# A transformer block on one Trainium2 core: a buffer of its own for a third partial sum, residual adds on another engine, earlier partial sums, earlier statistics of the first tile

## The chip, the core and the metric

The kernel runs on one core of one Trainium2 chip. The metric is the device time of that core in microseconds (us). A kernel is run several times in a job, beside the kernel before on the same chip; medians and ranges are over those runs. The engines are called PE (matmul; PEld is its weight load), DVE (the vector engine), ACT (the scalar engine), POOL (GpSimd) and SP (which here only issues transfers).

## The reference

One block: a modulation vector from `c`, LayerNorm, a two-dimensional Fourier filter, a residual, LayerNorm again, a SwiGLU feed-forward, a residual. x is 2048 x 640 in bf16, the feed-forward is 1728 wide.

```python
mod = (_silu(c) @ w_mod).reshape(c.shape[0], 6, 1, -1)        # sa, ca, ga, sb, cb, gb
h = _layernorm(x) * (1 + ca) + sa
x = x + ga * irfft2(rfft2(h) * (w_r + 1j * w_i))
h = _layernorm(x) * (1 + cb) + sb
x = x + gb * ((silu(h @ w_gate) * (h @ w_up)) @ w_down)
```

The kernel does the Fourier transforms as matmuls with tables. Both parts of the feed-forward use a Strassen-Winograd scheme: seven products for eight, paid for with sums on DVE. The rows are taken in chunks of 2, 4, 4, 4 and 2 tiles of 128. The first chunk is done plainly, the other four in seven *down pairs* (two tiles each): 2 + 2 + 2 + 1.

## The kernel before

`[...]` marks cuts. First the head: the statistics of a tile, and the order in which the first tiles are issued. The order matters: in the trace of this kernel POOL scales tile 0's table (L372, from `gscale(0)`) at 10.61 us, behind the power for tile 1 (L357, 9.94 to 10.50), which stands before it in the program, although tile 0's own power had ended at 8.34.

```python
def stats(t):
    if t in BN:                                   # by bn_stats on DVE (tiles 0 and 1 among them)
        for k in range(2):
            nc.vector.bn_stats(bn6a[:, k, :], x_sb[:, t, 320 * k:320 * k + 320])
        nc.vector.bn_aggr(mv[:, t, :], bn6a[:])
    else:
        gram_stats(t)
    [...]                                         # variance on DVE
        nc.gpsimd.tensor_tensor(rstd[:, tt], vtmp[:, tt], mhalf[:, 0:len(us)], ALU.pow)

def gscale(t):                                    # first table of tile t times its rstd, on POOL
    [...]
    nc.gpsimd.tensor_scalar(Gs[:, 0:2, :], Gtab[:, tg], rstd[:, t:t + 1], float(D) ** 0.5, ALU.mult, ALU.mult)
    nc.gpsimd.tensor_scalar(Gs[:, 2, :], Gtab[:, tg, 1, :], rstd[:, t:t + 1], -float(D) ** 0.5, ALU.mult, ALU.mult)

for r in range(4):
    nc.vector.tensor_scalar_mul(Rs[:, 1, r, :], Rp[:, 4, :], mask4[:, r:r + 1])   # waits for tab_R
[...]
t1(0)                                             # transposes of tile 0
stats(0)
[...]
t1(1)
stats(1)
gscale(0)
[...]
gscale(1)
nc.gpsimd.tensor_copy(sc_rep[:], sc_f[:].unsqueeze(2).to_broadcast([P, NC5, 128]))
[...]
s1(0, Zs.pop(0), Gss.pop(0))                      # PE: needs gscale(0)
```

Then the down pair. X, Y, Z and W are PSUM banks; S1 to S4 are DVE sums of the activations (`a_sum`), T1 to T4 prepared sums of weights. X collects three partial sums one after another, and each is copied out by ACT before the next.

```python
g21b, g22b = (rL.cut(1024 * i, [512]) for i in range(2))
cps_ = [rL.cut((2560, 10496, 0, 1280)[i], [320], F32) for i in range(4)]

def a_sum(ATc, j, i, ks=slice(0, HK)):            # one of S1..S4, for the 128-column blocks ks of 7
    [...]
    tt = nc.vector.tensor_tensor

def down_pair(ATc, t, j, nxt):
    [...]
    last = t + 2 == NT
    prod(X, A11, B11, True, ks=range(0, 6))
    prod(Z, A12, B21, True, ks=range(0, 2))
    prod(X, A11, B11, stop=True, ks=range(6, HK))
    nc.scalar.copy(cps_[0], X)
    nc.gpsimd.tensor_tensor(xa[:, 0:320], xa[:, 0:320], cps_[0], ALU.add)
    [...]
    prod(Y, S1, T1, True, True)
    nxt(0)
    nc.scalar.copy(cps_[1], Y)
    prod(X, S2, T2, stop=True)
    nxt(1)
    nc.scalar.copy(cps_[2], X)                    # the third partial sum
    nc.gpsimd.tensor_tensor(xb[:, 320:640], xb[:, 320:640], cps_[1], ALU.add)
    nc.gpsimd.tensor_tensor(xa[:, 320:640], xa[:, 320:640], cps_[2], ALU.add)
    [...]                                         # four more products and the stores

def h_sums(ci):                                   # DVE sums for the gate-up of the next chunk
    [...]
    tt(t1, b11, b12, ALU.subtract)
    tt(t3, b22, b12, ALU.subtract)
    tt(t2, b22, t1, ALU.add)
    tt(t4, t2, b21, ALU.subtract)
    nc.vector.tensor_scalar_mul(t2, t2, -1.0)
```

`cps_[2]` at byte 0 of `rL` lies over `g21b` and the start of `g22b`, the activated gates of the gate-up stage that goes before.

## Time and profile before

| | before |
|---|---|
| median of 3 runs | 255.58 us (255.17 to 255.83) |
| span of the profiled execution | 254.3 us |
| PE busy / DVE busy / POOL busy | 96% / 83% / 30% |
| PE idle before a third product of a down pair | 2 x 0.4 us |
| first matmul of the last pair to the end of the span | 11.42 us |

The page of the kernel before begins with span, busy us, share and number of instructions of each engine.

```profile
span 254.3 us, 6460 instructions
PE 245.3 (96%) x2513; PEld 200.1 (79%) x2513; DVE 212.0 (83%) x517; ACT 162.3 (64%) x299; POOL 77.4 (30%) x123
```

PE is all but full, and the change leaves its work as it is. So a gain can come only from a gap of PE, and there are few. The list of waits of the kernel before names them (PE's output, line, what it waited for, us in total, times, longest):

```profile
PE psum L897 <- ACT rL L919: 0.8, 2, 0.4
PE psum L570 <- DMA rM<-in_w_mod_dram: 0.7, 1, 0.7
...
PE psum L971 <- POOL rW L784: 0.4, 1, 0.4
...
PE psum L897 <- DVE rE L854: 0.3, 1, 0.3
```

The first line is the down pairs, the last is the last pair. The timeline of the kernel before around one of those two pairs (start, duration, engine, line, operation, out<-in, form; in brackets the idle time before it and what ended it):

```profile
177.26 1.00 DVE L1062 TENSOR_TENSOR rX<-rH,rL 128x512 bf16<-128x512 bf16 x1
177.29 1.12 PE L897 MATMUL psum<-rA,rE 128*128 128x320 bf16 x7
178.35 0.42 ACT L919 COPY rL<-psum 128x320 f32<-128x320 f32 x1 [1.39 <-DVE rX L1062]
178.83 1.11 PE L897 MATMUL psum<-rE 128*128 128x320 f16 x7 [0.42 <-ACT rL L919]
178.83 0.77 PEld L897 LDWEIGHTS <-rE 128*128 128x128 f16 x6 [0.62 <-issue]
```

ACT could have copied the third partial sum (L919) much earlier, but it waits until DVE (L1062) has read `g22b`, which lies in the same bytes. PE then waits for the copy.

The last pair on the kernel before's DVE timeline: the sums L854 to L860 stand between PE and its products.

```profile
244.96 0.75 DVE L854 TENSOR_TENSOR rE<-rX 128x128 f16<-128x128 bf16 x1
245.63 0.68 DVE L856 TENSOR_TENSOR rE<-rE,rX 128x768 f16<-128x768 f16 x2
246.24 1.35 DVE L860 TENSOR_TENSOR rE<-rX,rE 128x768 f16<-128x768 bf16 x2
247.51 1.38 DVE L858 TENSOR_TENSOR rE<-rX 128x768 f16<-128x768 bf16 x2
```

And on its POOL timeline, the residual adds that run beside them:

```profile
244.77 0.86 POOL L910 TENSOR_TENSOR rM<-rM,rL 128x320 f32<-128x320 f32 x1 [17.83 <-ACT rL L909]
246.62 0.88 POOL L920 TENSOR_TENSOR rM<-rM,rL 128x320 f32<-128x320 f32 x1 [0.99 <-ACT rL L916]
247.95 0.86 POOL L921 TENSOR_TENSOR rM<-rM,rL 128x320 f32<-128x320 f32 x1 [0.45 <-ACT rL L919]
```

Two sums (a row x2 has two) take 0.68 us where POOL is quiet, and 1.35 and 1.38 where a POOL add lies over them. The head, in the kernel before's POOL timeline and then its weight-load timeline:

```profile
9.94 0.56 POOL L357 TENSOR_TENSOR rstd<-vtmp,mhalf 128x1 f32<-128x1 f32 x1 [1.61 <-DVE vtmp L352]
10.61 0.48 POOL L372 TENSOR_SCALAR rE<-rE,rstd 128x256 bf16<-128x256 bf16 x1
```

```profile
11.13 0.10 PEld L396 LDWEIGHTS <-rE 128*128 128x128 bf16 x1 [0.23 <-POOL rE L372]
11.60 0.10 PEld L397 LDWEIGHTS <-rE 128*128 128x128 bf16 x1 [0.37 <-POOL rE L373]
```

The scaling of tile 0's table (L372) stands behind the power for tile 1 (L357), and the first s1 products wait for it twice.

### The profile page before, as it was taken

The numbers are of one execution on the slowest core, as the hardware profiler recorded it, in microseconds if no ns is written. First come the engines' busy times: TensorE is split into PE (matmuls) and PEld (weight loads), VectorE is DVE, ScalarE is ACT, GpSimd is POOL, SyncE is SP. The second block draws the span as 40 slices with busy tenths as digits, with TensorE's granted clock in tenths as the row PEclk, the third lists the DMA queues.
The fourth block names the chain that finished last, engine by engine and source line by source line (L and its number), as shares of the span: only waits on it lengthen the run. The fifth ranks groups of instructions, "written<-read, shape, count | busy, mean of one in ns | idle before, by whom it ended". The sixth has DMA issues, their size and how long they took to land.

```text
span 254.3 us, 6460 instructions
## 1 busy us (share of the span) xinstructions
PE 245.3 (96%) x2513; PEld 200.1 (79%) x2513; DVE 212.0 (83%) x517; ACT 162.3 (64%) x299; POOL 77.4 (30%) x123
## 2 busy tenths in 40 slices
PE   8999998989999999999999999999999999999994
PEld 3678868989789888688877778886678887679962
DVE  2889898978898997779997997879985888993895
ACT  3678757978788686778862577674357765235630
POOL 7487785954022804000003900002220000440021
PEclk9999999999999999999999999999999999999999
DMA  6999999999999899600005020004210000211001
GB/s 220 396 348 298 283 391 175 264 314 389 283 350 269 198 263 172 142 14 0 3 0 106 17 76 15 3 3 80 70 44 14 3 0 17 39 52 54 4 0 52
DMA packets 45760, 34.43 MB, mean 135 GB/s; under 512 B 21731, under 2 KB 42658, under 8 KB 45346
## 3 DMA queue, kind: packets, MB, share of 16 engines
q1 hardware_dynamic: 43936, 30.00, 42.5%
q0 software_dynamic: 1504, 3.95, 6.6%
q8 instruction: 19, 0.31, 0.5%
q10 hardware_dynamic: 290, 0.08, 0.1%
q14 instruction: 11, 0.09, 0.1%
HBM read 26.72 MB, written 4.72 MB: 124 GB/s over the span
## 4 chain that ended last, share of the span: by engine, by line
PE 69%; DVE 10%; DMA 7%; issue 5%; POOL 4%; SPq 2%; ACT 2%; ACTq 0%; DVEq 0%; POOLq 0%
PE psum L1013 31%; PE psum L897 14%; PE psum L983 8%; DMA rM<-in_w_mod_dram 3%; PE psum L877 3%; SPq L518 2%; DMA rW<-rL 2%; DMA rE<-tab_R 2%; PE psum L971 2%; PE psum L595 2%; PE psum L397 1%; PE psum L396 1%; POOL rW L784 1%; PE psum L317 1%; PE psum L314 1%
## 5 line engine op out<-in xcount | busy, mean ns | idle before, releaser
L1013 PEld LDWEIGHTS <-rW 128*128 128x128 bf16 (+1 forms) x528 | 46.9, 98 | 5.6 <-issue 0.2
L910 POOL TENSOR_TENSOR rM<-rM,rL 128x320 f32<-128x320 f32 x7 | 7.0, 1002 | 85.9 <-ACT rL L909 85.9
L1013 PE MATMUL psum<-rW 128*128 128x256 bf16 (+1 forms) x240 | 27.1, 259 | 0.0
L897 PEld LDWEIGHTS <-rE 128*128 128x128 f16 (+1 forms) x196 | 18.8, 97 | 10.2 <-issue 1.2
L897 PE MATMUL psum<-rE 128*128 128x320 f16 (+1 forms) x147 | 22.7, 299 | 1.3 <-ACT rL L919 0.8
L1013 PE MATMUL psum<-rY,rW 128*128 128x256 bf16 (+1 forms) x96 | 24.0, 259 | 0.0
L983 PE MATMUL psum<-rW 128*128 128x256 bf16 (+1 forms) x170 | 23.1, 291 | 0.0
L588 DVE TENSOR_TENSOR rM<-psum,rW 128x384 bf16<-128x384 f32 (+2 forms) x42 | 20.2, 544 | 3.0 <-PE psum L566 2.5
L983 PEld LDWEIGHTS <-rW 128*128 128x128 bf16 x170 | 16.6, 98 | 3.8
L1013 PEld LDWEIGHTS <-rE 128*128 128x128 f16 x192 | 17.3, 98 | 2.6 <-DVE rE L961 0.3
L1049 DVE TENSOR_TENSOR rH<-psum,rW 128x512 bf16<-128x512 f32 x21 | 14.5, 689 | 5.8 <-PE psum L1013 3.9
L897 PEld LDWEIGHTS <-rX 128*128 128x128 bf16 (+1 forms) x151 | 14.6, 97 | 5.4
L758 POOL TENSOR_TENSOR rstd<-rstd,mhalf 128x4 f32<-128x4 f32 (+2 forms) x4 | 4.7, 1186 | 45.9 <-ACT rL L919 38.1
L1045 ACT COPY rH<-psum 128x512 f32<-128x512 f32 x21 | 12.3, 585 | 9.8 <-PE psum L1013 7.9
L1067 DVE TENSOR_TENSOR rX<-rH,rL 128x512 bf16<-128x512 bf16 x21 | 8.9, 424 | 9.9 <-ACT rL L1065 9.8
L1052 ACT COPY rX<-psum 128x512 f32<-128x512 f32 x21 | 12.3, 587 | 6.5 <-PE psum L1013 6.5
L1053 DVE TENSOR_TENSOR rX<-psum,rX 128x512 f32<-128x512 f32 x21 | 14.4, 685 | 2.1 <-ACT rX L1052 1.9
L1039 ACT COPY rW<-psum 128x512 f32<-128x512 f32 x21 | 12.3, 585 | 6.0 <-PE psum L1013 6.0
L385 DVE SCALAR_TENSOR_TENSOR rE<-rE,mv,psum 128x648 bf16<-128x648 f32 (+1 forms) x17 | 14.2, 845 | 1.9 <-PE psum L317 1.5
L897 PE MATMUL psum<-rA,rX 128*128 128x320 bf16 (+1 forms) x98 | 15.6, 299 | 0.0
L1013 PE MATMUL psum<-rH,rW 128*128 128x256 f16 (+1 forms) x96 | 15.1, 259 | 0.1
L1013 PE MATMUL psum<-rE,rY 128*128 128x256 f16 (+1 forms) x96 | 15.1, 259 | 0.0
(195 smaller groups left out, 679.9 us busy)
## 6 DMA issues: line engine op xcount, KB each, us to landing
out_dram<-rA SPq DMA_DIRECT2D x31, 80.0 KB, 1.6
rM<-in_w_mod_dram SPq DMA_DIRECT2D x3, 800.0 KB, 9.7
rX<-in_A_x_dram SPq DMA_DIRECT2D x3, 640.0 KB, 7.0
rA<-in_B_w_down_dram SPq DMA_DIRECT2D x2, 960.0 KB, 10.7
rM<-in_w_mod_dram SPq DMA_DIRECT2D x1, 1600.0 KB, 7.9
rY<-in_B_w_gate_dram POOLq DMA_DIRECT2D x2, 768.0 KB, 6.9
rW<-in_B_w_gate_dram SPq DMA_DIRECT2D x2, 640.0 KB, 7.3
rW<-in_B_w_up_dram SPq DMA_DIRECT2D x2, 640.0 KB, 7.6
```

Source lines behind the costliest of these rows:

```text
L385: nc.vector.scalar_tensor_tensor(Zv[:, h], Cv[:, h], mv[:, t, 0:1], zps[:, h], ALU.mult, ALU.subtract)
L588: nc.vector.tensor_tensor(PP[:, :, hl], xv[:, :, hl], in1, ALU.mult)
L877: nc.tensor.matmul(pop, lhsT=ATc[rows(k), k, tl * 128:(tl + 1) * 128], rhs=Wd_sb[rows(k), k, 320 * h:320 * h + 320], start=(k == 0), stop= ...
L897: nc.tensor.matmul(o, lhsT=lhsT, rhs=rhs, start=start, stop=stop, skip_group_check=True)
L983: nc.tensor.matmul(gu[u], lhsT=Wgu[:, u, c5, ff * 128:(ff + 1) * 128], rhs=h2T[:, :, c5, :], start=(c5 == 0), stop=(c5 == NC5 - 1))
L1013: nc.tensor.matmul(o[:, f], lhsT=w, rhs=b, start=(start and f == 0 and i == 0), stop=(stop and f == F - 1 and i == len(ops) - 1), skip_gro ...
L1039: nc.scalar.copy(c0, X)
L1045: nc.scalar.copy(c2, X)
L1049: nc.vector.tensor_tensor(c11, Z, c0, ALU.add)
L1052: nc.scalar.copy(c3, X)
L1053: nc.vector.tensor_tensor(c22, Y, c3, ALU.add)
L1067: nc.vector.tensor_tensor(ato, v4(c11), v4(g21), ALU.mult)
```

## The change

Four things: (1) the third partial sum gets bytes of its own; (2) the residual adds of the last pair go to DVE, so that POOL doesn't hold up the sums, and a third of those sums is begun a step earlier; (3) `t3` is computed last in `h_sums`; (4) in the head, statistics of tile 0 go before the DVE work that waits for `tab_R`, `gscale(0)` before tile 1's statistics, and the copy `sc_rep` earlier; the first two groups of idle matmuls (`idle_pe`, which only keep PE running) have 4 and 4 in place of 6 and 3. The last step refactors `stats` into `bn`, `rstd_of` and `gram_stats`; that part is cut.

```diff
-    idle_pe(6)
+    idle_pe(4)
[... stats(t) split into bn(t) and rstd_of(us) ...]
-        idle_pe(3)
+        idle_pe(4)
[...]
+        bn(0)
         for r in range(4):
             nc.vector.tensor_scalar_mul(Rs[:, 1, r, :], Rp[:, 4, :], mask4[:, r:r + 1])
         nc.gpsimd.memset(SL[:], 0.0)
         nc.gpsimd.memset(SAx[:], 0.0)
+        nc.gpsimd.tensor_copy(sc_rep[:], sc_f[:].unsqueeze(2).to_broadcast([P, NC5, 128]))
[...]
+        rstd_of((0,))
         t1(0)
-        stats(0)
[...]
+        gscale(0)
         t1(1)
-        stats(1)
-        gscale(0)
+        bn(1)
+        rstd_of((1,))
[...]
         gscale(1)
-        nc.gpsimd.tensor_copy(sc_rep[:], sc_f[:].unsqueeze(2).to_broadcast([P, NC5, 128]))
[... the later stats(t) calls replaced by their parts, in the same places ...]
-    cps_ = [rL.cut((2560, 10496, 0, 1280)[i], [320], F32) for i in range(4)]
+    cps_ = [rL.cut((2560, 10496, 9216, 1280)[i], [320], F32) for i in range(4)]
[... down_pair ...]
+        add = (nc.vector if last else nc.gpsimd).tensor_tensor
[...]
-        nc.gpsimd.tensor_tensor(xa[:, 0:320], xa[:, 0:320], cps_[0], ALU.add)
+        add(xa[:, 0:320], xa[:, 0:320], cps_[0], ALU.add)
[...]
-        nc.gpsimd.tensor_tensor(xb[:, 320:640], xb[:, 320:640], cps_[1], ALU.add)
-        nc.gpsimd.tensor_tensor(xa[:, 320:640], xa[:, 320:640], cps_[2], ALU.add)
+        add(xb[:, 320:640], xb[:, 320:640], cps_[1], ALU.add)
+        add(xa[:, 320:640], xa[:, 320:640], cps_[2], ALU.add)
[... h_sums ...]
         tt(t1, b11, b12, ALU.subtract)
-        tt(t3, b22, b12, ALU.subtract)
         tt(t2, b22, t1, ALU.add)
         tt(t4, t2, b21, ALU.subtract)
         nc.vector.tensor_scalar_mul(t2, t2, -1.0)
+        tt(t3, b22, b12, ALU.subtract)
[... gate-up of the last chunk ...]
             step(2, p)
+            if n == 2 and p == 2:
+                for q in (0, 2, 1, 3):
+                    a_sum(ATc, 0, q, slice(0, 2))
             step(6, p - 1)
[...]
-            r1, r2, r3, r4 = (lambda q=q: a_sum(ATc, 0, q, slice(0, 6)) for q in range(4))
+            r1, r2, r3, r4 = (lambda q=q: a_sum(ATc, 0, q, slice(2, 6)) for q in range(4))
```

More of the change, by code (lines that the diff above doesn't have):

```diff
@@ L338, in t1, with bn, rstd_of @@
             hTs[t] = hT
-        def stats(t):
-            if t in BN:
-                for k in range(2):
-                    nc.vector.bn_stats(bn6a[:, k, :], x_sb[:, t, 320 * k:320 * k + 320])
-                nc.vector.bn_aggr(mv[:, t, :], bn6a[:])
-            else:
-                gram_stats(t)
-            if t % 2 == 1 or t == 0:
-                us = (t,) if t < 2 else (t - 1, t)
-                for u in us:
-                    if u in BN:
-                        nc.vector.tensor_scalar(vtmp[:, u:u + 1], mv[:, u, 1:2], EPS, float(D), ALU.add, ALU.mult)
-                for tt in ([slice(t - 1, t + 1)] if t not in BN and t - 1 not in BN else [slice(u, u + 1) for u in us if u not in BN]):
-                    nc.vector.scalar_tensor_tensor(vtmp[:, tt], mv[:, tt, 0], -float(D), mv[:, tt, 0], ALU.mult, ALU.mult)
-                    nc.vector.scalar_tensor_tensor(vtmp[:, tt], ssq[:, tt], EPS * D, vtmp[:, tt], ALU.add, ALU.add)
-                tt = slice(us[0], t + 1)
-                nc.gpsimd.tensor_tensor(rstd[:, tt], vtmp[:, tt], mhalf[:, 0:len(us)], ALU.pow)
+        def bn(t):
+            for k in range(2):
+                nc.vector.bn_stats(bn6a[:, k, :], x_sb[:, t, 320 * k:320 * k + 320])
+            nc.vector.bn_aggr(mv[:, t, :], bn6a[:])
+        def rstd_of(us):
+            bns = [u for u in us if u in BN]
+            for u in bns:
+                nc.vector.tensor_scalar(vtmp[:, u:u + 1], mv[:, u, 1:2], EPS, float(D), ALU.add, ALU.mult)
+            for tt in ([slice(u, u + 1) for u in us if u not in BN] if bns else [slice(us[0], us[-1] + 1)]):
+                nc.vector.scalar_tensor_tensor(vtmp[:, tt], mv[:, tt, 0], -float(D), mv[:, tt, 0], ALU.mult, ALU.mult)
+                nc.vector.scalar_tensor_tensor(vtmp[:, tt], ssq[:, tt], EPS * D, vtmp[:, tt], ALU.add, ALU.add)
+            tt = slice(us[0], us[-1] + 1)
+            nc.gpsimd.tensor_tensor(rstd[:, tt], vtmp[:, tt], mhalf[:, 0:len(us)], ALU.pow)
         def gram_stats(t):
@@ L457, in adaln_block_kernel @@
         gscale(1)
-        nc.gpsimd.tensor_copy(sc_rep[:], sc_f[:].unsqueeze(2).to_broadcast([P, NC5, 128]))
         t1(3)
-        stats(2)
+        gram_stats(2)
         zout(1)
@@ L463, in adaln_block_kernel @@
         t1(4)
-        stats(3)
+        gram_stats(3)
+        rstd_of((2, 3))
         dfwd(2)
@@ L471, in adaln_block_kernel @@
                 t1(t + 3)
-            if t + 2 < NT:
-                stats(t + 2)
+            u = t + 2
+            if u < NT:
+                (bn if u in BN else gram_stats)(u)
+                if u % 2:
+                    rstd_of((u - 1, u))
             if t > 3:
```

## The prediction

> **What bounds it now.** By the page's busy table PE works 96% of the 254.3 us span; DVE 83%, ACT 64%, POOL 30%; the granted clock is full throughout. Matmuls run back to back nearly everywhere, so only PE gaps can be won. The timeline shows them where the change works:
>
> 1. Head. PE's first dft waits 0.15 us for the scaled table (8.14), the first s1 matmuls 0.23 + 0.37 us for gscale of tile 0 (11.13, 11.60). That gscale stands on POOL behind tile 1's power, which waits for tile 1's bn_stats.
> 2. Two of the seven down pairs (178.4 and about 219.6): PE waits 0.4 us each (list of waits: 0.8 in 2) for ACT's copy of the third partial sum, which idles 1.39 us until DVE has read g22 with the last product: their buffers overlap in rL.
> 3. Last pair (242.9 to the end): 7.9 us of PE for about 6.8 us of matmuls. PE waits for the DVE sums (gaps 0.26, 0.16, 0.4 us). Sums of 128 columns take 752, 877 and 912 ns while POOL adds residuals, 214 ns where it doesn't. The Trainium skill ("SBUF — State Buffer", Who interferes with whom) says that a DVE instruction with two SBUF inputs and a GpSimd one that reads SBUF exclude each other; this trace agrees.
>
> **What the change does, costed.**
> - Own buffer for the third sum: copy starts about 0.9 us earlier, PE gap gone: -0.8 us. PE has no wait after it that could take this back (gate-up follows at full rate; its inputs have over 0.5 us of slack).
> - Last pair: the three POOL adds (0.86 us each) go to DVE, queued behind all sums. Estimate 0.40 us each, from the 128x320 DVE residual adds' pace of 0.40. DVE work there: +1.2 us adds, -1.8 us of blocked sums, -0.5 us because a third of four sums is done earlier. I expect PE to end about 1.1 us earlier, but DVE's backlog of adds and stores to hand back some: last DVE op about 0.85 us earlier (250.3, before 251.1). The final store keeps its 3 us.
> - Early sums: about 0.85 us DVE (0.2 each) near 238.5, where DVE idles 0.7 us. They may push the c22 add (ends 241.03; PE's next needs it at 241.09) by about 0.1 us: +0.1.
> - Head: bn_stats of tile 0 runs while DVE waited 1.06 us for tab_R, so one_p_ca starts about 0.35 us earlier; PE gains about 0.25, since tile 1's arrival (7.51) still bounds it. gscale(0) before bn(1) ends the 0.6 us wait. Part returns (tile 4's transposes need the gram bank and x; DVE is dense from 12.9 to 15.8): -0.6 us. sc_rep (0.72 us) moves ahead of the edge DMAs, not critical. The table stage after (SP transposes, w_mod load awaited at 52.9) is triggered by these results, so it should shift along.
> - Order of t3 in h_sums, fewer idle matmuls: 0.
>
> **Sum:** -0.8 - 0.75 - 0.6 = about -2.2 us: 253.4 us, range 252.6 to 254.6; faster by 2% 0.02, within 0.97, slower 0.01.
>
> **What would show it.** No PE wait for the third copy; DVE sums of the last pair at about 0.2/0.4 us, PE from the last pair's first matmul to its end about 6.9 us; no PE wait on POOL at 11 us; steady tile loop (t1 of tile 6, now 15.76) at about 15.2; w_mod wait at 52.9 about 0.6 us earlier, not longer.
>
> **What would make it wrong.** w_mod's landing at 52.9 bound by DMA bandwidth: the head gain becomes a longer wait (253.9). PE warming up later because c_row arrives after only four idle matmuls. x tiles 4 to 7 landing about 11 us, so PE waits for them. Early sums delaying PE by 0.4 us. POOL's adds of the other pairs, now earlier, blocking DVE longer.

## The result, and the profile after

| | before | after |
|---|---|---|
| median of 6 runs each | 255.71 us (255.17 to 256.67) | 252.26 us (251.96 to 253.00) |
| ratio after/before, 95% interval | | 0.9866 (0.9843 to 0.9889) |
| span of the profiled execution | 254.3 us | 251.2 us |
| PE idle before a third product of a down pair | 2 x 0.4 us | none |
| first matmul of the last pair to the end of the span | 11.42 us | 10.33 us |

A ratio here and below is the mean time of one kernel's fast runs over that of the other's of the same rounds, so it is not quite the ratio of the medians. All results were correct.

The kernel is 1.3% faster, within 2% as forecast, but 252.26 us lies below the predicted range (252.6 to 254.6). The forecast gain was too small. The page of the changed kernel:

```profile
span 251.2 us, 6466 instructions
PE 243.2 (97%) x2512; PEld 200.2 (80%) x2512; DVE 211.2 (84%) x524; ACT 162.6 (65%) x299; POOL 74.8 (30%) x120
```

Its list of waits has neither the third copy nor the DVE sums; at its head, after the warm-up, stand a load and what hangs on loads:

```profile
PE psum L572 <- DMA rM<-in_w_mod_dram: 0.8, 1, 0.8
PE psum L974 <- POOL rW L786: 0.7, 2, 0.4
```

To see where the time came from, I paired the matmuls of the two traces in order and took the difference of their starts. It is a running account: between two points it changes only where one kernel waits and the other doesn't. "First dft" is the first matmul that reads the scaled table, s1 the first product of a tile with the table that `gscale` makes, and the 13th column the last 64 columns of gate and of up, taken together.

| point (time before, us) | after minus before, us | step |
|---|---|---|
| first dft (8.1) | -0.64 | -0.64 |
| s1 of tile 0 done (12) | -1.14 | -0.22, -0.32 and small losses |
| matmul that waits for w_mod (52.9) | -1.10 | |
| gate-up of the 13th column (84.4) | -0.65 | +0.45 given back |
| gate-up of the third chunk (149.5) | -0.87 | -0.20 |
| first waiting down pair (178.8) | -1.45 | **-0.58** |
| second waiting down pair (219.6) | -2.03 | **-0.58** |
| last pair (245.8, 246.2, 248.1) | -2.98 | -0.42, -0.33, -0.18 |
| end of the span | -3.1 | |

**The down pairs.** The timeline of the changed kernel at the pair that was shown above:

```profile
176.40 0.99 DVE L1065 TENSOR_TENSOR rX<-rH,rL 128x512 bf16<-128x512 bf16 x1
...
176.68 0.43 ACT L922 COPY rL<-psum 128x320 f32<-128x320 f32 x1 [0.53 <-PE psum L899]
...
177.38 1.12 PE L899 MATMUL psum<-rE 128*128 128x320 f16 x7
```

The copy now starts during DVE's instruction, 0.28 us after it, and PE goes on without a break. Each of the two gaps gave 0.58 us, not the 0.42 that the list of waits showed.

The reason is how a gap is counted. In the trace, a 128x320 matmul lasts 299 ns and the next one starts 136 ns after it. So the row of a stream of matmuls overlaps itself by 163 ns, and "idle" is counted from the end of the last matmul, when the next has long been due. Before the change the starts are 177.973, 178.109 and then 178.827: 718 ns where 136 would do, hence 582 ns lost, of which 417 are shown as idle. The Trainium skill has both figures ("TensorE: Matmul & The Clock Gate", Single matmul latency: (398+N)/2.4 ns, 299 at N = 320; Back-to-back issue gap: N/2.4 + 2.5 ns, 136). This trace agrees with the second, 135 to 138 ns from start to start. The agreement with the first, 299 ns, confirms nothing, because the profile models the end of a matmul (its legend says so) and doesn't observe it.

**The last pair.** The DVE timeline of the changed kernel. The sums and then the three adds (L913, L923, L924):

```profile
242.83 0.23 DVE L856 TENSOR_TENSOR rE<-rX 128x128 f16<-128x128 bf16 x1
242.98 0.55 DVE L858 TENSOR_TENSOR rE<-rE,rX 128x512 f16<-128x512 f16 x2
243.45 0.55 DVE L862 TENSOR_TENSOR rE<-rX,rE 128x512 f16<-128x512 bf16 x2
243.92 0.55 DVE L860 TENSOR_TENSOR rE<-rX 128x512 f16<-128x512 bf16 x2
244.39 0.48 DVE L913 TENSOR_TENSOR rM<-rM,rL 128x320 f32<-128x320 f32 x1
244.79 0.48 DVE L923 TENSOR_TENSOR rM<-rM,rL 128x320 f32<-128x320 f32 x1
245.19 0.48 DVE L924 TENSOR_TENSOR rM<-rM,rL 128x320 f32<-128x320 f32 x1
```

Pairs of sums take 0.55 us each instead of up to 1.38, and the adds follow at a pace of 0.40, as was estimated. In the chain of waits of the changed kernel (start, us, what) the last pair is one piece of 53 matmuls, where before it alternated with DVE's sums:

```profile
239.93 1.09 PE psum L986 x10
241.02 6.76 PE psum L899 x53
...
```

From the first matmul of the last pair to the last is 6.67 us (before 7.69), to the last DVE operation 7.50 (8.52), to the end of the span 10.33 (11.42). DVE's backlog handed nothing back.

**`h_sums`.** Before, DVE (first fence) and PE (second):

```profile
149.15 0.29 DVE L961 TENSOR_SCALAR rE<-rE 128x512 f16<-128x512 f16 x1
```

```profile
149.50 0.61 PE L1013 MATMUL psum<-rE 128*128 128x256 f16 x4
```

After, the same:

```profile
148.28 0.29 DVE L963 TENSOR_SCALAR rE<-rE 128x512 f16<-128x512 f16 x1
148.49 0.42 DVE L964 TENSOR_TENSOR rE<-rW 128x512 f16<-128x512 bf16 x1
```

```profile
148.63 0.61 PE L1016 MATMUL psum<-rE 128*128 128x256 f16 x4
```

The negated `t2` was ready only at 149.44 and PE started at 149.50, 0.32 us after the matmul before it (149.18), where 0.11 is the pace. With `t3` behind it, it is ready at 148.57, and PE starts at 148.63, 0.12 us after the matmul before it. That is the step of -0.20, which the prediction had at nil.

**The head.** The scaled table of tile 0 is ready well before it is needed (changed kernel, POOL, then weight loads):

```profile
8.50 0.48 POOL L368 TENSOR_SCALAR rE<-rE,rstd 128x256 bf16<-128x256 bf16 x1 [1.37 <-DMA rE<-tab_G]
```

```profile
10.14 0.10 PEld L392 LDWEIGHTS <-rE 128*128 128x128 bf16 x1
10.20 0.10 PEld L393 LDWEIGHTS <-rE 128*128 128x128 bf16 x1
```

Both waits of the s1 products are gone. By 12 us the changed kernel leads by 1.14 us, twice the forecast; by 84 us it leads by 0.65. What of this is the change, and what is chance, could not be told from one pair of traces.

### The profile page after: what moved, and what is told of

It reads as the page before. It is cut to its first block, busy times and chain, and to the rows that moved or that the text cites. A ratio compares the mean times of both kernels' runs of the same rounds, so it can differ in the third digit from the quotient of the medians.

```text
span 251.2 us, 6466 instructions
## 1 busy us (share of the span) xinstructions
PE 243.2 (97%) x2512; PEld 200.2 (80%) x2512; DVE 211.2 (84%) x524; ACT 162.6 (65%) x299; POOL 74.8 (30%) x120
## 4 chain that ended last, share of the span: by engine, by line
PE 77%; DMA 8%; issue 4%; DVE 3%; SPq 3%; POOL 3%; ACT 1%; DVEq 0%; POOLq 0%; ACTq 0%
PE psum L1016 32%; PE psum L899 19%; PE psum L986 9%; DMA rM<-in_w_mod_dram 5%; PE psum L879 3%; DMA rW<-rL 3%; SPq L520 2%; PE psum L974 2%; PE psum L597 2%; PE psum L317 1%; PE psum L314 1%; PE psum L392 1%; PE psum L334 1%; PE psum L393 1%; POOL rW L786 1%
## 5 line engine op out<-in xcount | busy, mean ns | idle before, releaser
L913 POOL TENSOR_TENSOR rM<-rM,rL 128x320 f32<-128x320 f32 x6 | 5.9, 976 | 68.2 <-ACT rL L912 68.2
```

## The experiments

The theory after the result was: every step after 85 us is certain and comes from the three small edits there (0.20 + 1.16 + 1.09 = 2.45 us in place of the forecast 1.55); the head gives about as much as was forecast, with scatter by loads on top. Rivals: that the early copy `sc_rep` or chance of the loads and not the order of the statistics made the head faster (its worth below 0.3 us); that the adds on DVE or the early sums alone made the last pair; and that the time given back at 84 us is a limit of the loads which a better order of loads would lift. "Median" below is that of the kernel named; "before" the one of the kernel before in the same job.

### The changed kernel again, three times

No edit; three controls in three jobs, to see how much the changed kernel itself varies.

> Control: the changed kernel unaltered, for the baseline of this chip and a second trace. Every theory: ratio to the kernel before 0.985 to 0.988 (about 3.0 to 3.8 us faster). What I look at: start of each PE instruction against the trace of before. If the steps of the first changed trace are systematic, they come again: about -0.64 us at the first dft matmul, -1.1 us after the first s1 matmuls, +0.5 us given back at the 13th-column gate-up matmuls (83 us), -0.2 at 149 us, -0.58 at each of two down pairs, -0.95 in the last pair. Rival (run-to-run DMA luck): the -0.64 and the +0.5 differ by more than 0.3 us from these.

Measured: 252.9 us (251.89 to 254.03), before 255.61, ratio 0.9899 (0.9876 to 0.9922). Its trace has the same six steps after 85 us, within 0.02 us; but it leads by only 0.10 us at 84 us. Here the lead was lost at 52 us (1.15 us), where w_mod landed (its data was there) at 52.67 in place of 51.76, and hardly at 84 us (0.09 in place of 0.45): for the stretch before 85 us the rival, chance of the loads, holds.

> Control for the three runs of this call: the changed kernel unaltered. PE steps after 85 us as before: -0.20 at 149 us, -0.58 twice, and 10.33 us from the first matmul of the last pair to the end (11.42 in the kernel before). The place of the 13th-column gate-up matmuls (84 us) anywhere between 82.6 and 84.4 us.

Measured: 253.28 us, before 255.31, ratio 0.991 (0.9885 to 0.9935). The step at 149 us did not come as expected: PE lost 0.25 and 0.23 us at 142 to 144 us and 0.27 at 149, which the first trace and the other two controls of the changed kernel did not lose (see the last experiment).

> The changed kernel, partner of the next run on the same chip: 252.3 to 253.3 us.

Measured: 252.56 us, before 256.08, ratio 0.9847 (0.9806 to 0.9889). Over the four jobs that timed the changed kernel, the difference of medians is 3.45, 2.71, 2.03 and 3.52 us, mean 2.93. So the first result stood on the fortunate side of a scatter of about half a us.

### The third partial sum back over the gates

```diff
-    cps_ = [rL.cut((2560, 10496, 9216, 1280)[i], [320], F32) for i in range(4)]
+    cps_ = [rL.cut((2560, 10496, 0, 1280)[i], [320], F32) for i in range(4)]
```

> The changed kernel with only the third partial sum put back into the buffer that overlaps g21 and g22. Theory: PE loses 0.58 us, start to start, in each of the two pairs (1.16 us in all), as the trace of before shows, so +1.1 us; the list of waits will show only about 0.4 us each because it counts from the end of a matmul's latency. Rival (my forecast): 0.42 us each, +0.8 us. If something later absorbs it: under +0.5 us.

Measured: 254.25 us, before 255.61, ratio 0.9953 (0.9932 to 0.9974), 1.35 us more than the changed kernel of the same job. Its list of waits:

```profile
PE psum L899 <- ACT rL L922: 0.8, 2, 0.4
```

and its matmuls run 0.58 and 0.57 us later after the two pairs. So two waits that the list sums to 0.8 us cost 1.15 us: the undercount is shown by taking them away and putting them back. (This trace also lost 0.75 us between 142 and 149 us, as the second control did; that is not in the 1.15.)

### The last pair: adds back on POOL, and early sums taken out

```diff
-        add = (nc.vector if last else nc.gpsimd).tensor_tensor
+        add = nc.gpsimd.tensor_tensor
```

> The changed kernel with the three residual adds of the last pair back on POOL, the early sums kept. Theory (mutual exclusion of POOL and VectorE on two-input reads): VectorE's 128-column sums take 0.7 to 0.9 us again where POOL adds run, PE waits 0.6 to 0.9 us in the last pair, time +0.5 to +0.9 us. Rival (the gain of the tail came from the early sums, the adds only moved): under +0.3 us.

Measured: 253.65 us, before 256.03, ratio 0.9902 (0.988 to 0.9925). The DVE timeline has the long sums back, 1.22 and 1.21 us where the changed kernel has 0.55:

```profile
242.37 1.22 DVE L858 TENSOR_TENSOR rE<-rE,rX 128x512 f16<-128x512 f16 x2
243.51 1.21 DVE L862 TENSOR_TENSOR rE<-rX,rE 128x512 f16<-128x512 bf16 x2
```

First matmul of the last pair to the end: 10.81 us, 0.48 more than with the adds on DVE, of which PE lost 0.40; 0.5 to 0.9 was expected.

```diff
-            if n == 2 and p == 2:
-                for q in (0, 2, 1, 3):
-                    a_sum(ATc, 0, q, slice(0, 2))
[...]
-            r1, r2, r3, r4 = (lambda q=q: a_sum(ATc, 0, q, slice(2, 6)) for q in range(4))
+            r1, r2, r3, r4 = (lambda q=q: a_sum(ATc, 0, q, slice(0, 6)) for q in range(4))
```

> The changed kernel without the early sums (the sums of the last chunk whole again), adds on VectorE kept. Theory: each of four sums is about 0.13 us longer in the last pair and PE waits about 0.3 us for the second sum, time +0.2 to +0.4 us; the sums near 236.5 us cost nothing in the changed kernel, so nothing is won back there. Rival (the early sums delay the c22 add, as I forecast 0.1 us): PE's gate-up matmuls there begin about 0.1 us sooner without them and the loss is under 0.2 us.

Measured: 253.7 us, before 256.03, ratio 0.9894 (0.9872 to 0.9916). First matmul of the last pair to the end: 10.62 us, 0.29 more. At 236 to 241 us, where the early sums had stood and were forecast to cost 0.1, no matmul moves by over 0.06 us: the early sums were free.

So both halves pay, and neither alone explains the 1.09 us. Undone alone they cost 0.48 and 0.29; the remaining 0.32 is won as soon as either is in place, since each covers a part of the same waits. Medians of this job can't tell these differences apart (253.65, 253.7, 253.66, 253.85 for its four kernels, with no unaltered changed kernel among them); the traces, set against the first one of the changed kernel, can.

### `t3` back to second place

```diff
         tt(t1, b11, b12, ALU.subtract)
+        tt(t3, b22, b12, ALU.subtract)
         tt(t2, b22, t1, ALU.add)
         tt(t4, t2, b21, ALU.subtract)
         nc.vector.tensor_scalar_mul(t2, t2, -1.0)
-        tt(t3, b22, b12, ALU.subtract)
```

> The changed kernel with the t3 difference back in second place in the sums of h. Theory: -t2 is ready 0.3 us later and PE waits for it where the second chunk ends (step at 149 us of about 0.2 us, maybe 0.3 now that PE comes sooner), nowhere else: +0.2 to +0.3 us. Rival (my forecast): 0.

Measured: 253.66 us, before 256.03, ratio 0.9897 (0.9874 to 0.9921). In the trace +0.21 us at one place, the third chunk's gate-up (148.6 us), and nothing elsewhere. The 0.20 us is this line's.

### The head

The copy `sc_rep` back behind `gscale(1)`, the rest of the head kept:

```diff
-        nc.gpsimd.tensor_copy(sc_rep[:], sc_f[:].unsqueeze(2).to_broadcast([P, NC5, 128]))
         flip_edge(A_w_i, Wflip[0])
[...]
         gscale(1)
+        nc.gpsimd.tensor_copy(sc_rep[:], sc_f[:].unsqueeze(2).to_broadcast([P, NC5, 128]))
```

> The changed kernel with only the widening copy of silu(c) on POOL put back behind gscale of tile 1, so that the four edge DMAs on POOL's queue are issued at 2.9 us again and not at 4.1 us. Theory A (the copy holds the edge DMAs back, and that lets the first w_mod and table tiles land 0.35 us sooner): the first mod matmuls go back from 5.45 to about 5.8 us, the first dft from 7.50 to about 7.8 us, and the time rises by 0.2 to 0.4 us. Rival B (landing times vary by themselves, or come from the fewer idle matmuls): mod matmuls stay at 5.4 to 5.5 us, time unchanged within 0.1 us or moved the other way by POOL's later copy.

Measured: 252.51 us (5 runs), before 255.61, ratio 0.989 (0.9871 to 0.9908). The first modulation matmul starts at 5.21 us, no later than with the copy early: the copy is not the cause.

The whole head as before, all else changed (twice, in two jobs): the edit is the head's part of the diff above, undone.

```diff
-        bn(0)
[...]
-        rstd_of((0,))
         t1(0)
+        stats(0)
[...]
-        gscale(0)
         t1(1)
-        bn(1)
-        rstd_of((1,))
+        stats(1)
+        gscale(0)
[... idle_pe counts, sc_rep and the later stats calls as before ...]
```

> The changed kernel with the whole head of the kernel before (tile 0 statistics, order of gscale, copy of silu(c), idle matmuls), the rest kept. Theory: up to 45 us the head is worth 1.0 us (0.32 for VectorE freed before the scaled table, 0.40 for gscale, and 0.1 to 0.4 from landings that vary), so PE's first s1 matmuls are back at 11.1 and 11.6 us and the copy of the first mod_bc at about 39.7 to 40.1 us; but the DMA stream sets the waits at 52 and 83 us, and those landings differ by 1 us from run to run, so of the head only 0.3 to 0.8 us is left at 85 us and in the time. Rival (my forecast): all of it is carried through, 1.0 us or more slower than the changed kernel. Also a second trace of the old head: if its first w_mod lands at 5.1 to 5.4 us and not 5.77, the landing was luck of that trace.

Measured: 253.85 us, before 256.03, ratio 0.9909 (0.9891 to 0.9926). The two waits are back (weight loads, old head, second trace of it):

```profile
10.65 0.10 PEld L396 LDWEIGHTS <-rE 128*128 128x128 bf16 x1 [0.23 <-POOL rE L372]
11.11 0.10 PEld L397 LDWEIGHTS <-rE 128*128 128x128 bf16 x1 [0.36 <-POOL rE L373]
```

But they come 0.48 us earlier than in the trace of the kernel before (11.13, 11.60), whose head is the same. In that trace `tab_R` was first used at 5.67 us, later than in the others (4.74 to 5.34). The first dft comes at 7.72 us here and at 7.84 in the next run of the old head, against 8.14 there: about half of the 0.64 us was a late landing in that trace, and not the change. Against the first trace of the changed kernel this one is 0.66 us behind at 12 us but level with it from 84 us on (0.03 us), so a single pair of traces can also show no gain at all.

> The changed kernel with the old head, against its partner. Theory (the DMA waits at 52 and 83 us take most of the head): slower by under 0.3 us. Rival (my forecast of 0.6 us is carried through): slower by 0.5 to 0.8 us.

Measured, beside the third control on the same chip: 253.26 us against 252.56, ratios 0.9878 (0.9842 to 0.9914) and 0.9847 (0.9806 to 0.9889). The intervals overlap, so the times alone don't settle it. In the traces the old head is 0.58 us behind from 84 us to the end.

The best estimate comes from all traces with the same order of loads. The start of the 13th column's last gate-up matmul is 84.43, 83.80 and 83.97 us with the old head, mean 84.06, and between 82.63 and 84.33 with the new one, mean 83.32 of ten. The difference is 0.74 us. One trace scatters by about half a us, so the standard error of this difference is about 0.25 us: it agrees with the forecast -0.6 and speaks against a gain below 0.3, without excluding it. The whole 1.14 us seen at 12 us was not the change: the two later traces of the old head are 0.66 and 0.84 us behind there. The counts of idle matmuls were undone only together with the rest of the head.

### Are the loads the limit at 52 and 84 us?

Between the head and 84 us the lead varies from trace to trace. At two places PE waits for what was loaded: at 52 us for w_mod itself, at 83 for the gate-up of the 13th column, whose activations a DMA transposes and POOL then scales and shifts. Six kernels moved loads.

One gate-up load later:

```diff
     load_gu(0, 512)
-    load_gu(512, 1024)
[...]
                 ln2_tr(0)
+                load_gu(512, 1024)
                 load_gu(1024, 1664)
```

> The changed kernel with the second gate-up weight load (columns 512 to 1023 of gate and up, 1.28 MB) issued after the first LN2 transpose and not before it. Theory C: from 51 to 80 us the DMA engines are saturated, so the transpose, though issued 1.1 us sooner than before the change, lands only 0.4 us sooner behind those loads, and PE gives back 0.5 us at 83 us. Then here the transpose lands 1.5 to 3 us sooner (before 79.5 us), the PE wait on POOL's modulation at 83 us (0.40 and 0.27 us) is gone, and the time falls by 0.5 to 0.7 us; unless gate-up then waits for its weights at about 86 us. Rival D (the transpose's own length or POOL sets the 83 us wait): landing moves less than 0.3 us, no gain.

Measured: 258.1 us, before 255.61, ratio 1.0109 (1.0088 to 1.013): a miss. The wait at 83 us went (1.00 us from start to start against the first trace of the changed kernel). The columns moved landed at 84.9 us; but the last columns of `w_up`, which now come behind them, landed at 94.6 us instead of 86.4, and PE waited for those:

```profile
PE psum L985 <- DMA rW<-in_B_w_up_dram: 3.8, 1, 3.8
```

Half of the down weights behind the last gate-up load:

```diff
-    for h in range(2):
+    def load_wd(h):
         nc.sync.dma_start(Wd_sb[:, HK * h:HK * h + 6, :], [...])
+    load_wd(0)
[...]
                 load_gu(1024, 1664)
+                load_wd(1)
```

> The changed kernel with the second 0.96 MB of w_down loaded behind the last gate-up columns (after the first LN2 transpose), not ahead of all gate-up weights. Theory C again, without the fault of the earlier deferral: 0.96 MB less lie ahead of the transpose in a saturated DMA stream, about 2.5 to 3 us of it, so the transpose lands by 78.5 us and PE's wait for POOL's modulation at 83 us (0.2 to 0.7 us) goes; gate-up weights come sooner, not later; w_down's second half is not read before about 87 us. Time -0.3 to -0.6 us against the control, and the start of the 13th column at 84 us less scattered. Rival D (POOL or the transpose's own length sets it): no change.

Measured: 255.2 us, before 255.31, ratio 0.9979 (0.9951 to 1.0007). The wait at 83 us went here too: the transpose landed 3.9 us after its issue, in place of 6.6 in the first trace of the changed kernel. But DVE waited 3.5 us for the weights that it has to scale, and behind it PE lost 1.47 and 1.42 us from start to start (the list of waits gives 1.3 for each):

```profile
91.25 0.89 DVE L817 TENSOR_TENSOR rA<-rA,gb_bc 128x640 bf16<-128x640 bf16 x2 [3.51 <-DMA rA<-in_B_w_down_dram]
```

The load of w_mod split in two, the half needed first ahead:

```diff
-        nc.sync.dma_start(wm_r[:, :, 1:3, :], wm_m[:, :, 1:3, :])
+        nc.sync.dma_start(wm_r[:, :, 2, :], wm_m[:, :, 2, :])
+        nc.sync.dma_start(wm_r[:, :, 1, :], wm_m[:, :, 1, :])
```

> The changed kernel with the 1.6 MB load of w_mod columns awaited at 52 us split in two loads of 0.8 MB, the half that is used first loaded first. The PE wait of 0.7 to 1.0 us at 52 us goes. If the DMA stream is what sets the time at 84 us (theory C), PE then waits as much longer at 83 us, and the time stays within 0.3 us of the control; if not, it falls by 0.6 to 0.9 us.

Measured: 252.58 us (4 runs), before 255.31, ratio 0.9886 (0.9862 to 0.991). Set against the trace of the kernel before, PE gains 0.84 us at 52 us, gives back 0.47 at 54, where it waits for the other half, and 0.41 at 83. Nothing is left at 84 us, where this kernel is level with the control of its job (83.28 and 83.22 us): the gain turned into two later waits.

Both edits together:

> Both load changes on top of the changed kernel. Theory C: with the backlog ahead of the transpose gone, what PE wins at 52 us is carried through: -0.9 to -1.4 us against the control, more than the sum of the two alone. If the two simply add up: -0.3 to -0.8 us.

Measured: 254.67 us, before 255.31, ratio 0.9957 (0.9921 to 0.9994), with the same wait of DVE for the down weights. That is a miss too: 0.9 to 1.4 us less than the control was expected, and it is 1.4 us more.

The down weights between the gate-up loads, with the split w_mod, once with the new head and once with the old:

```diff
                 ln2_tr(0)
+                load_wd(1)
                 load_gu(1024, 1664)
```

> The changed kernel with the w_mod load split in two and the second 0.96 MB of w_down loaded after the first LN2 transpose but before the last gate-up columns (the earlier try had it after them, and VectorE waited 3.5 us for it). Theory C: no PE wait at 83 us, w_down's second half landed by 84 us, no VectorE wait at 87 us, gate-up columns in time at 90 us: 0.6 to 1.2 us faster than the changed kernel. Rival: the gate-up columns come too late and PE waits at 90 us: no gain or a loss.

> The same loads with the head of the kernel before. If the head is carried once the DMA waits are gone: 0.5 to 0.8 us slower than the run with the new head. If the DMA stream still sets the pace: under 0.3 us.

Measured: 252.28 us (new head) and 252.22 (old head), before 256.08, ratios 0.9843 (0.9805 to 0.9881) and 0.9844 (0.9807 to 0.9882); the changed kernel of the same job has 0.9847. The 0.6 to 1.2 us that were expected over the changed kernel did not come: the medians differ by 0.28 us and the intervals overlap. In the traces both loads' waits are gone (with the old head 0.2 us of the wait for w_mod is left), and the head's 0.59 us is there at 84 us (-2.46 against -1.87 us, each counted from the kernel before). By the end the new head's trace is 0.32 us behind the old one's, because it loses 0.11 us at 90 us and then 0.25, 0.23 and 0.27 at 142 to 149, in the way that the next experiment shows. The medians are level. So the loads do limit the stretch from 52 to 84 us, but no order tried was clearly faster than the changed kernel in time.

### A race of 20 ns between DVE and POOL

In every trace that has both, DVE's first sum of the second chunk and a POOL add start within 30 ns of each other, DVE first. In 14 of 18 traces (one of which is the third control, DVE and then POOL):

```profile
138.89 0.61 DVE L856 TENSOR_TENSOR rE<-rX 128x896 f16<-128x896 bf16 x1
138.92 1.31 POOL L923 TENSOR_TENSOR rM<-rM,rL 128x320 f32<-128x320 f32 x1
```

In the other four (the second control here; also the kernel with the buffer back, that with the down weights late, and that with new loads and the new head):

```profile
138.74 1.36 DVE L856 TENSOR_TENSOR rE<-rX 128x896 f16<-128x896 bf16 x1
138.76 0.85 POOL L923 TENSOR_TENSOR rM<-rM,rL 128x320 f32<-128x320 f32 x1
```

One of the two is held up for the other in each of the 18. Where it is DVE, PE loses 0.25 and 0.23 us at 142 to 144 us (shown as 0.09 and 0.07 us of idle time, again 0.16 us short) and 0.27 at 149, where the negated `t2` comes late. All four such traces have the new head (4 of 14); with the old head it is 0 of 4, too few to tell whether the change makes it more frequent. The Trainium skill ("SBUF — State Buffer", Who interferes with whom) says that a DVE instruction with two SBUF inputs and a POOL one that reads SBUF exclude each other, and that the one which issues first keeps the port while the other blocks. The durations agree; which of the two wins is here not settled by the start that the trace records.

Theory: with POOL out of the way this loss can't occur. Edit: adds of the first pair of every chunk on DVE.

```diff
-        add = (nc.vector if last else nc.gpsimd).tensor_tensor
+        add = (nc.vector if j == 0 else nc.gpsimd).tensor_tensor
```

> The changed kernel with the residual adds of the first pair of each chunk on VectorE too, not only of the last pair. Theory (which of VectorE and POOL, 20 ns apart, is first decides): the 896-column sums of chunk 1 take 0.6 us in place of 0.6 to 1.36, the two forms at 142 to 149 us are gone, and VectorE's 1.2 us of adds for each pair are about paid by 0.5 us less per blocked sum: time 0 to -0.5 us against the changed kernel, with no loss in any trace at 142 us. Rival (VectorE has no room, 94% busy in these stretches): PE waits for sums at 177 and 217 us, +0.3 us or more.

Measured: 252.43 us (251.93 to 253.33), before 255.81, ratio 0.9884 (0.986 to 0.9908). In the trace all four sums take 0.62 us and PE loses nothing at 142. The time does not differ from the changed kernel's, of whose four traces one has the loss; no unaltered kernel ran in this job.

> That, with the two reordered loads. If both effects hold: PE 1.0 to 1.3 us sooner than the changed kernel at 84 us and nothing lost at 142 us, so 251.2 to 251.8 us, the fastest of all.

This is that edit with the new order of loads. Measured: 252.87 us (251.38 to 254.23), before 255.81, ratio 0.9885 (0.985 to 0.9919). It has the lowest single time of all runs (251.38 us) and no better median. Its profiled execution (251.5 us) has both effects, 1.45 us ahead of the first trace of the changed kernel at 84 us and no loss at 142; the median of the six does not. No version clearly beats the changed kernel.

## Why the prediction was right or wrong

The forecast was -2.2 us. The sum of the steps now measured is -0.74 (head, mean) - 0.20 - 1.16 - 1.09 = -3.2 us, and the mean of four jobs is -2.9. Point by point, in the prediction's words:

- **"Own buffer for the third sum: [...] PE gap gone: -0.8 us."** The mechanism was right, the size wrong. The list of waits counts from the end of the last matmul, 163 ns after the next was due. Each gap was worth 0.58 us, both 1.16. Shown by the trace after, and by the kernel with the buffer back.
- **"I expect PE to end about 1.1 us earlier, but DVE's backlog of adds and stores to hand back some".** PE's end came 1.02 us earlier, as expected, and the backlog handed back nothing (last DVE operation also 1.02 us earlier, and not 0.85; end of span 1.09). The pace of the adds, 0.40 us, was estimated right. The Trainium skill ("GPSIMD Engine Reference", 4.1 Engine selection) has two-input elementwise work about twice as slow on GpSimd; here it is 0.86 us for an add on POOL against 0.48 on DVE, whose adds follow each other at a pace of 0.40. DVE had worked its backlog off by the next product: that ended at 246.24 and DVE took it at 246.28.
- **"Early sums: [...] +0.1."** They cost nothing measurable and gain 0.29 us.
- **"Order of t3 in h_sums, fewer idle matmuls: 0."** The order is worth 0.20 us. The negated `t2` gated a matmul at one place, the third chunk's gate-up. I had looked for slack at another place, the chunk that begins at 186 us, and took it for all. The kernel with the old order shows it.
- **"Part returns [...]: -0.6 us"** (head). Right in the mean as far as the scatter lets one say, 0.74 with a standard error of about 0.25, though one trace shows anything from 0.1 to 1.8 us. The lead of 1.14 us at 12 us is in part a late landing in the one trace of before.
- **"w_mod wait at 52.9 about 0.6 us earlier, not longer".** Half right: it ended 1.10 us earlier, but the wait itself grew from 0.68 to 0.84 us. The loads there land when they land: a part of the head's lead is lost to them in some executions and not in others.
- **Hazards named.** No wait for `c_row` or for the x tiles 4 to 7 appears in the list of waits after. "POOL's adds of the other pairs [...] blocking DVE longer" exists in 4 of 18 traces and costs PE 0.75 us there. It is not shown to be a result of the change: the trace of the kernel before has the same two starts 0.03 us apart.

So the error of about 0.9 us is in three terms of the sum: the two down pairs 0.36 (idle time taken for the cost of a wait), the last pair 0.34 (a backlog and a delay that cost nothing), `h_sums` 0.20 (a nil where PE waited). The head was right within its scatter. The first result stood some 0.5 us on the lucky side besides; the mean of the four medians of the changed kernel is 252.75 us, just inside the range. The range was set as if the terms could err by little and mostly upward.

## What to carry to other kernels

When a wait of PE is costed from a profile, take the distance of the starts around it less the pace of the stream, not the idle time that a list of waits gives: at 128x320 that is 0.16 us more for each gap. Check every consumer of a reordered value, not one instance, before writing a nil. And a gain that passes through a stretch limited by loads can't be read from one pair of traces: take the mean of several.

## What the Trainium skill lacked or had wrong

- "Perfetto Trace Analysis", Optimization Strategy, tells the reader to find the gaps between slices on the engine. It doesn't say that on PE such a gap is short by the length shown for a matmul less its pace: 299 - 136 = 163 ns at 128x320, so that a gap shown as 0.42 us was worth 0.58.
- "TensorE: Matmul & The Clock Gate", Back-to-back issue gap, gives about 81 ns a matmul at N = 128 and 131 at N = 512 for a real stream with a weight load before every matmul, and calls N/2.4 + 2.5 the isolated figure. In these traces such streams run at 56 ns (N = 128) and, in groups of five, 216 ns (N = 512) from start to start: the isolated formula held in the real stream.
- "SBUF — State Buffer", Who interferes with whom, says that issue order decides who blocks. With two starts 20 to 30 ns apart, DVE first in the record each time, POOL was held up in 14 of 18 traces (0.61 us for DVE) and DVE in 4 (1.36 us). The page has nothing on such near ties.
- "DMA: Bandwidth & Descriptors" gives bandwidth by size and a few latencies, but no scatter between executions. The same 1.6 MB load in the same order of loads took between 7.29 and 8.65 us from issue to landing in 13 traces.
